# Second layer of the last three token blocks by seven products of halves

## The chip, the cores and the metric

The kernel runs on one core of one Trainium2 chip. A core has five engines with queues of their own: TensorE (PE in the profile; its weight loads are listed apart as PEld), VectorE (DVE), ScalarE (ACT), GpSimd (POOL) and SyncE (SP, here only DMA issues). TensorE multiplies into PSUM, which has 8 banks of 2 KB in each of 128 partitions; the other engines work on SBUF, and VectorE and ScalarE on PSUM too. Each engine takes its queue in order; semaphores hold an instruction back until what it depends on is done. The metric is device time in microseconds (us), less is better.

## The reference

Two stages follow each other: an attention over 8 batches, 8 heads, 576 positions and 64 columns a head, and a feed-forward pair of matrices over the 4608 x 512 tokens that come out of it.

```
q_d, k_d, v_d = means of 4 neighbouring positions          # 144 coarse positions
out_up    = repeat(softmax(q_d k_d^T / 8) v_d, 4)          # coarse attention
out_local = softmax(q k^T / 8 where |i - j| < 4) v         # band attention
x = (out_up + out_local) as 4608 tokens x 512
h = x @ w_in                                               # 512 -> 2048
g = where(h > 0, h, exp(min(h, 0)) - 1)
out = g @ w_out                                            # 2048 -> 512
```

## The kernel before, in words

All matmul operands are fp16, sums are fp32. The tokens are cut into 9 blocks of 512 (t = 0 to 8). A batch of attention has 576 tokens, so the attention of batch b feeds blocks b and b + 1 in part; batch 7 feeds the last 64 tokens of block 7 and the whole of block 8.

For a block, the first layer is `mm1(t, i)`, i = 0 to 15: four matmuls of 512 columns (line 719) make 128 of the 2048 hidden features for the 512 tokens in one PSUM bank called hp. ScalarE takes exp of it (line 723), VectorE turns that into min(e, 1) - 1 (line 724) and adds max(h, 0) from the bank (line 725); the result is one of 16 slices of the tile gt. There are two hp banks. The second layer is `mm2(t, i)`, i = 0 to 15: four matmuls of 512 columns each (line 739), sixteen for each quarter of 128 tokens, which add up in a bank of the tag misc (two banks). ScalarE copies the quarter to an os tile (line 745), and SP sends it out (line 747). The last quarter of block 8 is made in two parts of 384 and 128 columns.

The attention of a batch works on four pairs of heads (j = 0 to 3). GpSimd casts the loaded q, k and v to fp16 (lines 241, 302) and sums q; TensorE transposes q (line 328) and makes scores (lines 458, 471) in two-bank tiles called two0, two1 (and two2 at the front); ScalarE takes their exps (line 481), VectorE masks them (line 496) and sums k (line 377); TensorE adds up denominators (line 518), then makes the outputs lg (lines 602, 622), again in two-bank tiles. VectorE multiplies them by the reciprocals (lines 666, 671), and GpSimd adds the coarse part and writes the block's input xt (line 683).

The order of all of this is written out by hand. Every piece of work is put on a list with a time (`at(time, fn, ...)`), the list is sorted by time, and the pieces are issued in that order; each engine's queue thus has the order of the list, and the times have no other meaning. `mm1_at(t, i)` is i steps behind the start of block t, and blocks start 16 steps apart; `mm2_at(t, i)` is half a step behind `mm1_at(t + 1, i)`. So from block 3 on TensorE alternates between four matmuls of the first layer of block t + 1 and four of the second layer of block t, and the pieces of the attention lie between them at offsets given for each batch (the tables LATER, and LAST for batch 7). The second layer of block 8 has nothing beside it.

PSUM is full: two banks misc, two hp, four in two0 and two1. SBUF is one pool, sb.

## Time and profile before

| | |
|---|---|
| median of 3 runs | 352.85 us |
| lowest, highest run | 350.0, 353.14 us |
| profiled execution: span from the first to the last instruction | 353.6 us |
| TensorE busy | 335.8 us (95%) |
| VectorE, ScalarE, GpSimd busy | 236.2, 180.6, 160.0 us |
| mean granted TensorE clock | 0.981 |
| first layer, line 719 | 512 matmuls, 133.7 us busy |
| second layer, line 739 | 592 matmuls, 146.0 us busy |

Busy time is the time in which an engine has an instruction under way. Matmuls overlap in the pipeline, so the time of one (some 380 ns for 512 columns) is longer than the distance between two; distances are read from starts. In the order of time, "x4" is a merged row of four like instructions, whose length reaches from the first start to the last end; what stands in brackets is the engine's idle time before it and what ended it. "L719" is line 719 of the kernel before.

### The profile page before, as it was taken

How to read it: one execution, taken by the hardware profiler on the slowest of the kernel's cores; microseconds unless marked ns; L12 is line 12 of the kernel's file. 1: busy time of each engine (PE TensorE's matmuls, PEld its weight loads, DVE VectorE, ACT ScalarE, POOL GpSimd, SP SyncE). 2: the span in 40 equal slices, each digit the busy share in tenths (PEclk: the TensorE clock that was granted, in tenths of full speed). 3: DMA queues.
4: the chain of work that ended last, by engine and by line, in shares of the span. 5: the costliest groups of instructions: out<-in, count | busy, mean ns of one | idle time of the engine just before them, and what ended most of it. 6: DMA issues, size and time to landing. Idle time of an engine off the chain costs nothing.

```text
span 353.6 us, 10486 instructions
## 1 busy us (share of the span) xinstructions
PE 335.8 (95%) x4288; PEld 185.3 (52%) x4288; DVE 236.2 (67%) x466; ACT 180.6 (51%) x312; POOL 160.0 (45%) x298
## 2 busy tenths in 40 slices
PE   8897998899889998899999999999999999999996
PEld 4665784455455544445555555545455544444443
DVE  2316999665878775977797789779756955555510
ACT  3572795256665653466355636663553444444421
POOL 4563458286875841973396449755300600000000
PEclk9998999879989999999999999999999999999999
DMA  9999997899998869898979797953014010010012
GB/s 177 201 209 192 213 208 152 200 213 190 188 185 158 167 139 181 168 190 158 196 150 214 158 214 155 168 131 54 30 35 116 32 59 31 32 52 37 32 59 89
DMA packets 98768, 48.89 MB, mean 138 GB/s; under 512 B 81617, under 2 KB 93217, under 8 KB 98721
## 3 DMA queue, kind: packets, MB, share of 16 engines
q1 hardware_dynamic: 94417, 41.86, 58.7%
q0 software_dynamic: 4064, 6.26, 10.0%
q8 instruction: 33, 0.54, 0.7%
q10 hardware_dynamic: 240, 0.11, 0.2%
q14 instruction: 14, 0.11, 0.1%
HBM read 41.97 MB, written 9.55 MB: 146 GB/s over the span
## 4 chain that ended last, share of the span: by engine, by line
PE 75%; DVE 13%; DMA 6%; issue 3%; ACT 3%; SPq 0%; DVEq 0%; ACTq 0%
PE op L739 31%; PE hp L719 28%; DVE gt L725 4%; DMA rcb<-rd 3%; DVE e L724 3%; DVE ln L671 2%; DMA rd<-rc 2%; PE sc L758 2%; PE tqk L328 2%; PE sc L458 2%; PE lg L602 1%; ACT e L723 1%; PE vs L405 1%; PE lg L622 1%; PE den L518 1%
## 5 line engine op out<-in xcount | busy, mean ns | idle before, releaser
L739 PE MATMUL op<-WO,gt 128*128 128x512 f16 (+2 forms) x592 | 146.0, 375 | 0.5 <-DVE gt L725 0.5
L723 ACT ACTIVATE e<-hp 128x512 f16<-128x512 f32 x144 | 86.2, 599 | 107.1 <-PE hp L719 95.3
L719 PE MATMUL hp<-xt,WI 128*128 128x512 f16 x512 | 133.7, 385 | 1.4 <-DVE gt L725 1.3
L725 DVE SCALAR_TENSOR_TENSOR gt<-hp,e 128x512 f16<-128x512 f32 x144 | 99.6, 692 | 6.4
L724 DVE TENSOR_SCALAR e<-e 128x512 f16<-128x512 f16 x144 | 60.6, 421 | 58.4 <-ACT e L723 58.0
L739 PEld LDWEIGHTS <-gt 128*128 128x128 f16 x592 | 55.4, 98 | 61.7 <-issue 1.6
L719 PEld LDWEIGHTS <-WI 128*128 128x128 f16 x512 | 55.6, 115 | 50.0 <-issue 3.2
L683 POOL TENSOR_TENSOR xt<-ln 128x128 f16<-128x128 f16 (+7 forms) x55 | 36.6, 693 | 56.9 <-DVE ln L671 56.9
L481 ACT ACTIVATE pex<-sc 128x580 f16<-128x580 f32 (+1 forms) x56 | 30.1, 594 | 9.2 <-PE sc L471 8.6
L302 POOL CAST v<-v 128x640 f16<-128x640 f32 (+1 forms) x32 | 23.7, 741 | 20.4 <-DMA v<-in_v_dram 13.6
L394 POOL TENSOR_TENSOR t<-qt 128x288 f32<-128x288 f16 x27 | 18.1, 670 | 31.4 <-ACT qt L358 31.4
L745 ACT COPY os<-op 128x512 f32<-128x512 f32 (+2 forms) x37 | 21.4, 578 | 18.9 <-PE op L739 18.8
L377 DVE TENSOR_REDUCE ke<-kt 128x145 f16<-128x580 f16 x28 | 21.0, 751 | 2.4 <-ACT kt L365 2.4
L358 ACT COPY qt<-tqk 128x576 f16<-128x576 f16 x28 | 17.9, 639 | 8.4 <-PE tqk L328 7.7
L671 DVE TENSOR_TENSOR ln<-lg,rcb 128x580 f16<-128x580 f32 x28 | 21.1, 752 | 0.0
L241 POOL CAST k<-k 96x768 f16<-96x768 f32 x24 | 19.8, 825 | 0.1
L241 POOL CAST q<-q 96x768 f16<-96x768 f32 x24 | 19.6, 818 | 0.0
L698 PE MATMUL hp<-xt,WI 128*128 128x256 f16 x128 | 17.0, 283 | 0.7 <-DVE v L276 0.4
L496 DVE TENSOR_TENSOR pex<-pex,MASK 128x580 f16<-128x580 f16 x28 | 13.6, 486 | 3.0 <-ACT pex L481 2.8
L698 PEld LDWEIGHTS <-WI 128*128 128x128 f16 x128 | 13.3, 116 | 1.9 <-issue 0.8
L396 POOL TENSOR_TENSOR qd<-t 128x144 f16<-128x144 f32 x27 | 12.1, 448 | 2.1
L458 PEld LDWEIGHTS <-kt 64*64 64x64 f16 x560 | 6.9, 109 | 11.2 <-issue 8.6
(113 smaller groups left out, 273.4 us busy)
## 6 DMA issues: line engine op xcount, KB each, us to landing
out_dram<-os SPq DMA_DIRECT2D x35, 256.0 KB, 2.1
v<-in_v_dram SPq DMA_DIRECT2D x111, 80.0 KB, 4.5
q<-in_q_dram SPq DMA_DIRECT2D x25, 288.0 KB, 3.9
...
```

The source lines that it names most:

```text
L241: nc.gpsimd.tensor_copy(out=x[:], in_=src)
L302: nc.gpsimd.tensor_copy(out=v16[:], in_=v32[:].rearrange("p (e c) d -> p c e d", e=2))
L481: nc.scalar.activation(out=s["p"][:, :, a : a + n], in_=g2(sc, a, n), func=AF.Exp, scale=SCALE / 16 if a else SCALE,)
L671: nc.vector.tensor_tensor(out=ln[:, 0 : 2 * WL].rearrange("p (m h u) -> p m h u", h=2, u=WQ), in0=_free(lg[:, 0:1], [[WQ, WM], [512, 2], [ ...
L683: eng.tensor_tensor(out=xt(t)[:, j, t0 - TBLK * t : t1 - TBLK * t], in0=ln[:, a:z], in1=_rep4(ln[:, ga : ga + (z - a) // 4]), op=AB.add,)
L698: nc.tensor.matmul(FS[i][:, 256 * f : 256 * f + 256], w_in(dc, 2 * n + f), xts[0][:, dc, 256 * h : 256 * h + 256], start=(f == dc == 0), s ...
L719: nc.tensor.matmul(hp, w_in(dc, fc), xts[t][:, dc, :], start=(dc == 0), stop=(dc == DMC - 1),)
L723: nc.scalar.activation(out=e, in_=hp, func=AF.Exp)
L724: nc.vector.tensor_scalar(out=e, in0=e, scalar1=1.0, scalar2=-1.0, op0=AB.min, op1=AB.add)
L725: nc.vector.scalar_tensor_tensor(out=to, in0=hp, scalar=0.0, op0=AB.max, in1=e, op1=AB.add)
L739: nc.tensor.matmul(op_[:, a:z], gts[t][:, fc, 128 * tt : 128 * tt + 128], WO[:, fc, a:z], start=(fc == 0), stop=(fc == FCN - 1),)
L745: nc.scalar.copy(out=os_[:, a:z], in_=op_[:, a:z])
```

## The change

For the blocks t = 6, 7 and 8 (SW = 6) the second layer is made in another way. The block's 512 x 2048 activations g are taken as 2 x 2 halves, by tokens (256) and hidden features (1024), and w_out as 2 x 2 halves by hidden features (1024) and columns (256). Seven products of halves, with sums and differences of the halves as factors, give the four quarters of the output (Winograd's form of Strassen's scheme) where eight products would be needed:

- `weights_7`: four differences of the halves of w_out, in eight VectorE subtractions of 128 x 1024 fp16 elements, listed from 0.6 steps after the last casts of batch 7, every 2 steps.
- `sums_7(t, g)`: four sums and differences of the halves of g for a quarter g of the features, 128 x 512 elements each, on GpSimd (the last group of block 8 on VectorE). One of the four is written in place in gt. They are listed behind `mm1(t, 4 g + 3)`; the third group of block 6 stands behind the last outputs of batch 7. So that both halves of the features come together, the first layer of these blocks makes slices 0, 8, 1, 9, ...
- `product(t, u, n)`: eight matmuls of 256 columns for 128 of the 256 tokens of a half (u = 0, 1). Products 1, 6, 5 and 3 add up in the left half of a bank y, one after the other, and what stands there in between is read by ScalarE (copies after 1 and 6) and VectorE; products 2, and 7 and 4, go to the two halves of a misc bank.
- `finish(t, u, n)`: after products 4 and 5 a VectorE addition, after 3 a ScalarE copy, make the output rows, and SP sends them.

For blocks 6 and 7 the products stand in the order 1, 2, 7, 6, 4, 5, 3 at 0, 1, 2, 3, 4, 5 and 7 steps of each half block, the finishes of 4 and 5 0.6 steps behind, that of 3 0.1 steps behind. For block 8 they follow each other directly.

In blocks 7 and 8, ten of sixteen slices (i % 8 in BELOW) get their activation from two ScalarE instructions, r = Relu(-h) and e = Exp(-r), and one of VectorE, max(e - 1, h).

When the last outputs of batch 7 are made, the banks of two0 and two1 go back (`close_attention`) and become two banks y and two banks hx; hx takes half of the slices of the first layer of blocks 7 and 8. The SBUF tiles that are needed up to the last casts and transposes of batch 7 are in two pools of their own (lo, tu), which are closed there (`close_feed`, `close_turn`); the differences, sums and output tiles take their place.

```
+SW = 6
+BELOW = (1, 2, 5, 6, 7)
...
+    feed = ctx.enter_context(ExitStack())
+    turn = ctx.enter_context(ExitStack())
+    lo = feed.enter_context(tc.tile_pool(name="lo", bufs=1, side="right"))
+    tu = turn.enter_context(tc.tile_pool(name="tu", bufs=1))
...
+    pairs_ = ctx.enter_context(ExitStack())
+    tp = pairs_.enter_context(tc.tile_pool(name="tp", bufs=1, space=bass.MemoryType.PSUM))
+    fp = front.enter_context(tc.tile_pool(name="fp", bufs=1, space=bass.MemoryType.PSUM, side="right"))
     late = {}
...
     def bank(tag, name):
-        pool = late["ps"] if tag == "hp" else ps
+        pool = {"hp": late["ps"], "misc": ps}.get(tag) or late["end"]
         return pool.tile([128, 512], FP32, tag=tag, bufs=2, name=name)
...
-    def mm1(t, fc):
+    def mm1(t, i):
+        fc = i if t < SW else i // 2 + 8 * (i % 2)
         if fc == 0:
             gts[t] = sb.tile([128, FCN, TBLK], FP16, tag="gt", bufs=2, name="gt")
         e = sb.tile([128, TBLK], FP16, tag="e", bufs=3, name="e")[:]
             h, n = divmod(fc, 8)
             to = gts[t][:, 2 * n : 2 * n + 2, 256 * h : 256 * h + 256]
         else:
-            hp, to = bank("hp", "hp")[:], gts[t][:, fc, :]
+            hp = bank("hx" if t > SW and i % 4 > 1 else "hp", "hp")[:]
+            to = gts[t][:, fc, :]
             for dc in range(DMC):
                 nc.tensor.matmul(
                     hp, w_in(dc, fc), xts[t][:, dc, :],
                     start=(dc == 0), stop=(dc == DMC - 1),
                 )
+        if t > SW and i % 8 in BELOW:
+            r = sb.tile([128, TBLK], FP32, tag="os", bufs=3, name="r")[:]
+            nc.scalar.activation(out=r, in_=hp, func=AF.Relu, scale=-1.0)
+            nc.scalar.activation(out=e, in_=r, func=AF.Exp, scale=-1.0)
+            nc.vector.scalar_tensor_tensor(
+                out=to, in0=e, scalar=-1.0, op0=AB.add, in1=hp, op1=AB.max
+            )
+            return
         nc.scalar.activation(out=e, in_=hp, func=AF.Exp)
         nc.vector.tensor_scalar(out=e, in0=e, scalar1=1.0, scalar2=-1.0, op0=AB.min, op1=AB.add)
         nc.vector.scalar_tensor_tensor(
 
     def mm2(t, i):
         tt, part = i // 4, i % 4
-        cols = ((0, DM),)
-        if t == NT - 1 and tt == 3:
-            cols, part = ((0, 384), (384, DM)), 0
-        for a, z in cols:
-            if part == 0:
-                ops[(t, tt)] = bank("misc", "op")
-            op_ = ops[(t, tt)]
-            for fc in range(4 * part, 4 * part + 4 if len(cols) == 1 else FCN):
-                nc.tensor.matmul(
-                    op_[:, a:z], gts[t][:, fc, 128 * tt : 128 * tt + 128], WO[:, fc, a:z],
-                    start=(fc == 0), stop=(fc == FCN - 1),
-                )
-            if part == 3 or len(cols) == 2:
-                os_ = sb.tile([128, DM], FP32, tag="os", bufs=3, name="os")
-                nc.scalar.copy(out=os_[:, a:z], in_=op_[:, a:z])
-                r = TBLK * t + 128 * tt
-                nc.sync.dma_start(out=out[r : r + 128, a:z], in_=os_[:, a:z])
+        if part == 0:
+            ops[(t, tt)] = bank("misc", "op")
+        op_ = ops[(t, tt)]
+        for fc in range(4 * part, 4 * part + 4):
+            nc.tensor.matmul(
+                op_[:], gts[t][:, fc, 128 * tt : 128 * tt + 128], WO[:, fc, :],
+                start=(fc == 0), stop=(fc == FCN - 1),
+            )
+        if part == 3:
+            os_ = sb.tile([128, DM], FP32, tag="os", bufs=3, name="os")
+            nc.scalar.copy(out=os_[:], in_=op_[:])
+            r = TBLK * t + 128 * tt
+            nc.sync.dma_start(out=out[r : r + 128], in_=os_[:])
...
+    W7, S7, U7 = {}, {}, {}
+    MH, TH, FH = DM // 2, TBLK // 2, FCN // 2
+    def close_feed():
+        feed.close()
+        late["w"] = ctx.enter_context(tc.tile_pool(name="w7", bufs=1, side="right"))
+        W7["T"] = late["w"].tile([128, 4, FH, MH], FP16, tag="T", name="w7")
+    def close_turn():
+        turn.close()
+        late["s"] = ctx.enter_context(tc.tile_pool(name="s7", bufs=1))
+    def weights_7(n, c):
+        T, k = W7["T"], slice(4 * c, 4 * c + 4)
+        b11, b12 = WO[:, k, 0:MH], WO[:, k, MH:DM]
+        b21, b22 = WO[:, FH + 4 * c :, 0:MH][:, 0:4], WO[:, FH + 4 * c :, MH:DM][:, 0:4]
+        x, y = ((b12, b11), (b22, T[:, 0, k]), (b22, b12), (b21, T[:, 1, k]))[n]
+        nc.vector.tensor_tensor(out=T[:, n, k], in0=x, in1=y, op=AB.subtract)
+    def sums_7(t, g):
+        if g == 0:
+            S7[t] = late["s"].tile([128, 3, FH, TH], FP16, tag="S", bufs=2, name="s7")
+        S, G, k, l = S7[t], gts[t], slice(2 * g, 2 * g + 2), slice(FH + 2 * g, FH + 2 * g + 2)
+        a11, a12, a21, a22 = G[:, k, 0:TH], G[:, l, 0:TH], G[:, k, TH:TBLK], G[:, l, TH:TBLK]
+        eng = nc.vector if (t, g) == (NT - 1, 3) else nc.gpsimd
+        for to, x, y, op in (
+            (S[:, 0, k], a21, a22, AB.add), (a21, a11, a21, AB.subtract),
+            (S[:, 1, k], S[:, 0, k], a11, AB.subtract), (S[:, 2, k], a12, S[:, 1, k], AB.subtract),
+        ):
+            eng.tensor_tensor(out=to, in0=x, in1=y, op=op)
+    def close_attention():
+        pairs_.close()
+        late["end"] = ctx.enter_context(tc.tile_pool(name="end", bufs=1, space=bass.MemoryType.PSUM))
+    def unit(t, u):
+        if (t, u) not in U7:
+            z, y = bank("misc", "xz"), bank("y", "y")
+            sn = late["s"].tile([128, 3, MH], FP32, tag="sn", bufs=2, name="sn")
+            ou = late["s"].tile([128, 2, DM], FP32, tag="ou", bufs=2, name="ou")
+            U7[(t, u)] = z, y, sn, ou
+        return U7[(t, u)]
+    def product(t, u, n, k0=0, k1=FH):
+        xz, y, sn, ou = unit(t, u)
+        G, S, T = gts[t], S7.get(t), W7["T"]
+        a, b = slice(128 * u, 128 * u + 128), slice(TH + 128 * u, TH + 128 * u + 128)
+        to = y[:, 0:MH] if n in (1, 3, 5, 6) else xz[:, 0:MH] if n == 2 else xz[:, MH:DM]
+        for k in range(k0, k1):
+            w, x = (
+                (G[:, k, a], WO[:, k, 0:MH]), (G[:, FH + k, a], WO[:, FH + k, 0:MH]),
+                (S[:, 2, k, a], WO[:, FH + k, MH:DM]), (G[:, FH + k, b], T[:, 3, k]),
+                (S[:, 0, k, a], T[:, 0, k]), (S[:, 1, k, a], T[:, 1, k]), (G[:, k, b], T[:, 2, k]),
+            )[n - 1]
+            nc.tensor.matmul(
+                to, w, x, start=(k == 0 and n in (1, 2)), stop=(k == FH - 1),
+                skip_group_check=n > 2,
+            )
+        if k1 == FH and n in (1, 6, 7):
+            nc.scalar.copy(out=sn[:, {1: 0, 6: 1, 7: 2}[n], :], in_=to)
+    def finish(t, u, n):
+        xz, y, sn, ou = unit(t, u)
+        to = y[:, 0:MH]
+        r, z = TBLK * t + 128 * u, TBLK * t + TH + 128 * u
+        if n == 4:
+            nc.vector.tensor_tensor(
+                out=ou[:, :, 0:MH], in0=xz[:].rearrange("p (c m) -> p c m", c=2), in1=sn[:, 0:2, :],
+                op=AB.add,
+            )
+        if n == 5:
+            nc.vector.tensor_tensor(out=ou[:, 1, MH:DM], in0=to, in1=sn[:, 2, :], op=AB.add)
+            nc.sync.dma_start(out=out[z : z + 128], in_=ou[:, 1, :])
+            if (t, u) == (NT - 1, 1):
+                nc.sync.dma_start(out=out[r : r + 128, 0:MH], in_=ou[:, 0, 0:MH])
+        if n == 3:
+            nc.scalar.copy(out=ou[:, 0, MH:DM], in_=to)
+            m0 = MH if (t, u) == (NT - 1, 1) else 0
+            nc.sync.dma_start(out=out[r : r + 128, m0:DM], in_=ou[:, 0, m0:DM])
...
-            if 16 * t + i <= 16 * NT - 4:
+            if t < SW:
                 at(mm2_at(t, i), mm2, t, i)
+    at(PLAN[B - 1]["cast"][3] + 0.05, close_feed)
+    at(PLAN[B - 1]["tr"][3] + 0.05, close_turn)
+    for n in range(4):
+        for c in range(2):
+            at(PLAN[B - 1]["cast"][3] + 0.6 + 2 * (2 * n + c), weights_7, n, c)
+    for t in range(SW, NT):
+        for g in range(4):
+            x = mm1_at(t, 4 * g + 3) + 0.05
+            if (t, g) == (SW, 2):
+                x = max(x, max(PLAN[B - 1]["out"]) + 0.1)
+            at(x, sums_7, t, g)
+        z = mm2_at(t, 0)
+        if t < NT - 1:
+            for u in range(2):
+                for n, x in zip((1, 2, 7, 6, 4, 5, 3), (0, 1, 2, 3, 4, 5, 7)):
+                    at(z + 8 * u + x, product, t, u, n)
+                    if n in (4, 5, 3):
+                        at(z + 8 * u + x + (0.1 if n == 3 else 0.6), finish, t, u, n)
+        else:
+            steps = [(u, n, 0, FH - 1) for u in range(2) for n in (1, 2)]
+            steps += [(u, n, FH - 1, FH) for u in range(2) for n in (1, 2)]
+            steps += [(u, n) for u, n in ((0, 7), (0, 6), (1, 7), (1, 6), (0, 4), (0, 5), (1, 4), (1, 5), (0, 3), (1, 3))]
+            for n, x in enumerate(steps):
+                at(z + n, product, t, *x)
+                if x[1] in (4, 5, 3):
+                    at(z + n + 0.1, finish, t, *x)
+    at(mm1_at(SW + 1, 0) - 0.1, close_attention)
```

More of the change, by code (lines that the diff above doesn't have):

```diff
@@ L120, in const @@
     def const(a, name, queue):
-        t = C[name] = sb.tile(list(a.shape), FP16, tag=name, bufs=1, name=name)
+        pool = sb if name in ("ID", "MASK", "IND2", "VR2") else lo
+        t = C[name] = pool.tile(list(a.shape), FP16, tag=name, bufs=1, name=name)
         queue.dma_start(out=t[:], in_=nc.inline_tensor(a, name=name + "c").ap())
+    feed = ctx.enter_context(ExitStack())
+    turn = ctx.enter_context(ExitStack())
+    lo = feed.enter_context(tc.tile_pool(name="lo", bufs=1, side="right"))
+    tu = turn.enter_context(tc.tile_pool(name="tu", bufs=1))
     front = ctx.enter_context(ExitStack())
     ps = ctx.enter_context(tc.tile_pool(name="ps", bufs=1, space=bass.MemoryType.PSUM))
-    fp = front.enter_context(tc.tile_pool(name="fp", bufs=1, space=bass.MemoryType.PSUM))
+    pairs_ = ctx.enter_context(ExitStack())
+    tp = pairs_.enter_context(tc.tile_pool(name="tp", bufs=1, space=bass.MemoryType.PSUM))
+    fp = front.enter_context(tc.tile_pool(name="fp", bufs=1, space=bass.MemoryType.PSUM, side="right"))
     late = {}
@@ L136, in two @@
         turns.append(turns.pop(0))
-        pool = fp if turns[-1] == 2 else ps
+        pool = fp if turns[-1] == 2 else tp
         return pool.tile([128, 1024 if dt == FP32 else 2048], dt, tag=f"two{turns[-1]}", bufs=1, name=name)
     def bank(tag, name):
-        pool = late["ps"] if tag == "hp" else ps
+        pool = {"hp": late["ps"], "misc": ps}.get(tag) or late["end"]
         return pool.tile([128, 512], FP32, tag=tag, bufs=2, name=name)
@@ L147, in close_front @@
         late["ps"] = ctx.enter_context(
-            tc.tile_pool(name="late", bufs=1, space=bass.MemoryType.PSUM)
+            tc.tile_pool(name="late", bufs=1, space=bass.MemoryType.PSUM, side="right")
         )
@@ L175, in load_wo @@
         nc.gpsimd.dma_start(out=WO[:, 4 * n : 4 * n + 4, :], in_=src)
-    KD = [sb.tile([128, 2 * KG + 16], FP16, tag=f"kd{i}", bufs=1, name="kd") for i in range(4)]
+    KD = [lo.tile([128, 2 * KG + 16], FP16, tag=f"kd{i}", bufs=1, name="kd") for i in range(4)]
     KE = [sb.tile([128, 192], FP16, tag=f"ke{i}", bufs=1, name="ke") for i in range(4)]
@@ L244, in cast_qk @@
         qk16[(b, j)] = got[:: 1 if b < FLIP else -1]
-    V00 = sb.tile([KW, 2 * NB, D], FP32, tag="v32", bufs=3, name="v32")
+    V00 = lo.tile([KW, 2 * NB, D], FP32, tag="v32", bufs=3, name="v32")
     def load_v(b, j):
@@ L253, in load_v @@
             return
-        t = V00 if (b, j) == (0, 0) else sb.tile([KW, 2 * NB, D], FP32, tag="v32", bufs=3, name="v32")
+        t = V00 if (b, j) == (0, 0) else lo.tile([KW, 2 * NB, D], FP32, tag="v32", bufs=3, name="v32")
         def part(p0, p1, i0, i1):
@@ L272, in load_windows @@
     def load_windows(b, j, a):
-        t = sb.tile([128, 2 * WM, D], FP32, tag="v32", bufs=3, name="v32")
+        t = lo.tile([128, 2 * WM, D], FP32, tag="v32", bufs=3, name="v32")
         if b == 1:
@@ L391, in sums @@
         else:
-            t2 = sb.tile([128, 2 * SD], FP32, tag="pex", bufs=2, name="t2")
+            t2 = tu.tile([128, 2 * SD], FP32, tag="pex", bufs=2, name="t2")
             at_ = src.rearrange("p (g f) -> p f g", f=2)
@@ L750 @@
     act, dve = nc.scalar.copy, nc.vector.tensor_copy
-    Z = sb.tile([128, 512], FP16, tag="Z", bufs=1, name="Z")
+    Z = lo.tile([128, 512], FP16, tag="Z", bufs=1, name="Z")
     def keep(t, n):
@@ L826, in selections @@
         else:
-            src = sb.tile([KW, 16], FP16, tag="I4", bufs=1, name="I4")
+            src = lo.tile([KW, 16], FP16, tag="I4", bufs=1, name="I4")
             nc.vector.tensor_reduce(
@@ L830, in selections @@
             )
-            t = C[name] = sb.tile([KW, 1024], FP16, tag=name, bufs=1, name=name)
+            t = C[name] = lo.tile([KW, 1024], FP16, tag=name, bufs=1, name=name)
             parts, step = ((0, 8, 0),), 8
```

12 lines of the change are left out of this document (6 added, 6 removed).

## The prediction

> **What bounds the kernel now.** I read the page's busy times first, then the stretches of the last third, then the order of time in one steady step.
>
> ```profile
> PE 335.8 (95%) x4288; PEld 185.3 (52%) x4288; DVE 236.2 (67%) x466; ACT 180.6 (51%) x312; POOL 160.0 (45%) x298
> ```
>
> TensorE (PE) leads, but a share of the whole span says nothing of blocks 6 to 8, so I cut the end into stretches. The columns are PE, weight load, VectorE (DVE), ScalarE (ACT), GpSimd (POOL), then the granted clock.
>
> ```profile
> 240.00:260.00 20.00, 19.94 (x258) 10.39 (x258) 16.27 (x32) 10.15 (x18) 7.64 (x12) 1.00 0.12 42
> 260.00:281.50 21.50, 21.50 (x286) 11.19 (x285) 15.37 (x31) 8.82 (x15) 5.16 (x8) 1.00 0.23 62
> 281.50:309.10 27.60, 27.60 (x130) 13.46 (x129) 15.84 (x33) 11.91 (x20) 0.16 (x1) 1.00 0.10 39
> 309.10:336.70 27.60, 27.60 (x129) 13.44 (x128) 15.75 (x33) 11.91 (x20) 0.00 (x0) 1.00 0.10 39
> 336.70:353.60 16.90, 14.03 (x81) 7.15 (x79) 0.97 (x2) 3.09 (x6) 0.00 (x0) 1.00 0.21 78
> ```
>
> The reader should see that PE has no gap from 260 to 336.7 us, at full clock, while POOL is idle from 281.5 on. Whatever shortens PE there shortens the kernel, and any new wait on PE lengthens it by its full length: nothing is left to absorb it.
>
> ```profile
> 268.88 1.03 PE L719 MATMUL hp<-xt,WI 128*128 128x512 f16 x4
> 269.74 1.03 PE L739 MATMUL op<-WO,gt 128*128 128x512 f16 x4
> 269.94 0.60 ACT L723 ACTIVATE e<-hp 128x512 f16<-128x512 f32 x1 [1.13 <-PE hp L719]
> 270.57 0.29 DVE L724 TENSOR_SCALAR e<-e 128x512 f16<-128x512 f16 x1 [0.71 <-ACT e L723]
> 270.61 1.03 PE L719 MATMUL hp<-xt,WI 128*128 128x512 f16 x4
> 270.90 0.69 DVE L725 SCALAR_TENSOR_TENSOR gt<-hp,e 128x512 f16<-128x512 f32 x1
> 281.46 0.81 PE L719 MATMUL hp<-xt,WI 128*128 128x512 f16 x3
> 334.99 1.03 PE L719 MATMUL hp<-xt,WI 128*128 128x512 f16 x4
> ```
>
> One step is four first-layer and four second-layer matmuls: 270.61 - 268.88 = 1.73 us, 0.865 for each four, 0.216 for a matmul of 512 columns. Activation starts 0.20 after the four end. The last first-layer step, mm1(8,15), starts at 334.99; 31 steps of 1.727 earlier, at 281.46, is mm1(7,0), from which the second layer of block 6 follows.
>
> **Term 1, fewer columns.** A block's second layer goes from 64 matmuls of 512 columns to 7 products x 8 matmuls x 2 halves = 112 of 256. What one of 256 costs has two neighbours in the trace.
>
> ```profile
> 51.06 1.06 PE L698 MATMUL hp<-xt,WI 128*128 128x256 f16 x8
> L698 PE MATMUL hp<-xt,WI 128*128 128x256 f16 x128 | 17.0, 283 | 0.7 <-DVE v L276 0.4 <-DVE gt L725 0.3
> 350.01 0.50 PE L739 MATMUL op<-WO,gt 128*128 128x128 f16 x6
> L739 PE MATMUL op<-WO,gt 128*128 128x128 f16 x16 | 1.1, 219 | 0.0
> L698 PEld LDWEIGHTS <-WI 128*128 128x128 f16 x128 | 13.3, 116 | 1.9 <-issue 0.8
> L739 PEld LDWEIGHTS <-gt 128*128 128x128 f16 x592 | 55.4, 98 | 61.7 <-issue 1.6
> ```
>
> L698's eight follow each other every (1.06 - 0.28) / 7 = 0.111 us, with weight loads of 116 ns; the products load from gt-like tiles (98 ns). The 128-column ones follow every (0.50 - 0.219) / 5 = 0.056, closer than a load is long, so loads overlap. Between 0.056 and 0.216, halfway by columns, lies 0.109, which I take: 112 x 0.109 = 12.2 against 64 x 0.216 = 13.8, so 1.6 a block and **-4.8 us** in three (ends: 0.108, which is half of 0.216, gives -5.2; 0.111 gives -4.2). The Trainium skill speaks against small matmuls: TensorE: Matmul & The Clock Gate, section Back-to-back issue gap, gives about 81 ns for 128 columns and 131 for 512 in a stream with its loads. By an estimate between them (98 ns) the change would lose 112 x 98 - 64 x 131 = 2.6 us a block; the 56 and 216 ns above contradict both figures, so it gets no chance.
>
> **Term 2, product 3 waits for its own bank.** This is the step on which I decide. Products 1, 6, 5 and 3 add up in one bank y, and VectorE's finish of product 5 must read y before product 3 writes it. By their times, product 5 is queued at step 5.5 of a half block, mm1 of step 6 at 6.0, that finish at 6.1, mm1 of step 7 at 7.0, product 3 at 7.5 (step 6.5 has no product). VectorE takes its queue in order, so the finish stands behind the activation of step 6. Step 6 (and 14, in the second half) is one of those that now go through two ScalarE instructions before VectorE's. From the end of its matmuls: 0.20 to ScalarE, 0.60 for Relu and 0.60 for Exp (as L723), 0.69 for VectorE, then the finish. That has 256 columns from PSUM:
>
> ```profile
> L671 DVE TENSOR_TENSOR ln<-lg,rcb 128x580 f16<-128x580 f32 x28 | 21.1, 752 | 0.0
> L666 DVE TENSOR_TENSOR ln<-lg,rcb 128x144 f16<-128x144 f32 x28 | 8.4, 300 | 6.2 <-DMA rcb<-rd 3.9 <-PE lg L622 2.2
> ```
>
> (752 - 300) / 436 = 1.04 ns a column, so 300 + 112 x 1.04 = 416 ns. The chain is 0.20 + 0.60 + 0.60 + 0.69 + 0.42 = 2.5, and PE has only mm1 of step 7 (0.865) to cover it: 1.65, with the hand-over to PE 1.7 us of idle PE. Queued behind it on PE is everything else: mm1 of the next step, then all products. It happens twice in block 6 and twice in block 7: **+6.8** (ends 6.0, if the two ScalarE instructions take 0.5 each, and 8.0, if a copy of 0.3 stands ahead of them). Block 8's products come with no mm1 between, its finishes directly behind them with two other products (1.7 us) as cover against 0.2 + 0.42: no wait.
>
> **Term 3, product 7 of block 6 waits for POOL.** The last sums of block 6 are queued on POOL behind the last additions of the attention.
>
> ```profile
> 279.00 2.66 POOL L683 TENSOR_TENSOR xt<-ln 128x64 f16<-128x64 f16 x4 [1.84 <-DVE ln L671]
> L683 POOL TENSOR_TENSOR xt<-ln 128x512 f16<-128x512 f16 x4 | 4.3, 1070 | 0.0
> L302 POOL CAST v<-v 128x640 f16<-128x640 f32 x28 | 20.4, 729 | 12.6 <-DMA v<-in_v_dram 12.5
> 274.50 2.66 POOL L683 TENSOR_TENSOR xt<-ln 128x64 f16<-128x64 f16 x4 [18.88 <-DVE ln L671]
> 275.22 0.75 DVE L724 TENSOR_SCALAR e<-e 128x512 f16<-128x512 f16 x1
> ```
>
> POOL is free at 281.66. Each group of sums is four instructions of 512 elements, 1.07 each; product 7's seventh matmul needs the second of the last group, so six: 281.66 + 6.42 = 288.1. Beside POOL's work L724 takes 0.75 instead of 0.29 (last two rows): one of the two waits for the other. Two L724 in that time cost POOL up to 0.6: 288.7. PE reaches that matmul at 281.46 + 3 x 0.865 + 2 x 0.87 + 6 x 0.109 = 286.45: **+2.3**. Ends: 0, if a two-input sum went at the one-input rate of L302 (0.58, six end at 285.2); 3.0, if more L724 get between. Blocks 7 and 8 are covered: POOL's 4.3 us a group fits four steps of 1.73 twice over. Of this lock the Trainium skill says (SBUF — State Buffer, Who interferes with whom) that VectorE in a two-port mode, or with two SBUF inputs, shares one port pair with GpSimd and the later one waits for the whole instruction. The 0.75 agrees; by it the subtractions of term 4 wait too.
>
> **Term 4, the weights' differences on VectorE.** Eight subtractions of 1024 elements, placed at steps between mm1(5,12) and mm1(6,10). Nearest row:
>
> ```profile
> L496 DVE TENSOR_TENSOR pex<-pex,MASK 128x580 f16<-128x580 f16 x28 | 13.6, 486 | 3.0 <-ACT pex L481 2.8
> 242.73 0.76 DVE L724 TENSOR_SCALAR e<-e 128x512 f16<-128x512 f16 x1
> 246.34 1.03 PE L739 MATMUL op<-WO,gt 128*128 128x512 f16 x4
> 246.68 0.69 DVE L725 SCALAR_TENSOR_TENSOR gt<-hp,e 128x512 f16<-128x512 f32 x1
> 247.43 1.02 PE L719 MATMUL hp<-xt,WI 128*128 128x512 f16 x4
> 248.02 0.69 DVE L725 SCALAR_TENSOR_TENSOR gt<-hp,e 128x512 f16<-128x512 f32 x1
> 249.15 1.03 PE L719 MATMUL hp<-xt,WI 128*128 128x512 f16 x4
> ```
>
> 486 ns for 580 elements makes at most 0.86 for 1024; with a fixed part of 0.15 (L666: 300 - 144 x 1.04) it is 0.74. The first comes ahead of the L724 at 242.73, the second ahead of the L725 at 248.02. PE already waits at 247.43 for the L725 that ends at 247.37, so the first goes through whole, 0.74; the second finds 249.15 - 248.71 = 0.44 of slack: 0.3 more. The other six meet VectorE's gap of 0.71 a step; where block 6's first sums keep POOL busy they overfill it a little, 0.3 in all. **+1.3** (ends 0 and 2.5).
>
> **Term 5, the end.** The last copy has 256 columns, between these, and its transfer 128 KB.
>
> ```profile
> 349.92 0.48 ACT L745 COPY os<-op 128x384 f32<-128x384 f32 x1 [2.01 <-PE op L739]
> 350.81 0.27 ACT L745 COPY os<-op 128x128 f32<-128x128 f32 x1 [0.41 <-PE op L739]
> out_dram<-os SPq DMA_DIRECT2D x9, 256.0 KB, 2.0
> out_dram<-os SPq DMA_DIRECT2D x1, 64.0 KB, 1.5
> ```
>
> 0.375 for 0.27, and 1.65 for 1.5: **+0.25** (0.1 to 1, if the transfers before it are still running).
>
> **At nothing:** the four single-bank tiles, since PE waits for no bank from 260 on (the rows above); ScalarE's extra Relu and small copies, 13 x 0.6 + 4 x 0.38 = 9.3 us in the 13.8 of eight steps; VectorE has less, not more, after 281.5. If their cover went, it would show as PE waiting for hp.
>
> The **sum** is -4.8 + 6.8 + 2.3 + 1.3 + 0.25 = +5.9 us. On this execution, whose span is 353.6 us, that is 359.5; the median of the runs is 0.7 below that span, so I forecast **358.8**. By the terms' ends, not all at once, 355 to 362.5.
>
> **Rivals.** (a) Product 3 doesn't wait. Its place is y, its price the whole of term 2, and it decides at 0.865 us: if VectorE reached the finish before mm1 of step 6, as its 0.71 of idle time a step would allow, the chain is 0.2 + 0.42 and hidden. Then -0.9: 351.9, not slower. Against it stands only the order of the queue. Chance 0.10. (b) Beside that, POOL and VectorE also hide terms 3 and 4, as their half-idle rows after 260 suggest: -4.5, 348.3, faster. Against: both are busy just before 281.5. 0.08. (c) The new gaps make the clock drop. It did so here after gaps:
>
> ```profile
> 66.00:67.00 1.00, 0.55 (x28) 0.41 (x27) 1.00 (x3) 0.00 (x0) 0.00 (x0) 1.00 0.78 167
> 69.00:70.00 1.00, 1.00 (x29) 0.59 (x29) 0.00 (x0) 0.00 (x0) 0.96 (x2) 0.50 1.07 228
> ```
>
> After a stretch with PE 55% busy the granted clock is 0.50. The wait of 2.3, with 1.7 following, is such a stretch; 3.4 us at half clock would add 1.7, twice 3.4: about 361 to 363. 0.12. (d) 256-column matmuls cost so much more than 0.111 that nothing is saved: inside the main range unless over 0.123. Left to the forecast with its range: 0.70.
>
> **Numbers.** 1% is 3.5 us, about what a measurement of this kernel can tell from no change (its three runs lie 3.1 apart): faster is below 349.3, slower above 356.4. Faster has (b), 0.08; within 1% has (a) and 0.08 of the main case, where terms 3 and 4 both come out near zero (353 to 356.4): 0.18; slower the rest, 0.74. The range takes in the main case and one drop of the clock and leaves out (a) and (b): 352.8 to 363.
>
> **What would show it.** PE idle four times for 1.5 to 2 us before product 3, released by VectorE's addition; once for about 2.3 at a product 7, released by POOL; starts of product matmuls 0.109 apart; block 8's second layer 12.2 long with no gap. If PE stays gapless from 281 on, terms 2 and 3 are wrong and the time is (b)'s.

## The result, and the profile after

The changed kernel is slower: its median is 362.92 us (four runs, 361.57 to 363.74) against 351.48 for the kernel before beside it (four runs, 350.0 to 353.14). The ratio is 1.0339, with a 95% interval of 1.0277 to 1.04. The forecast was 358.8, +5.9 on 352.85; slower was right, and the time lies just inside the range, but the loss is about twice the forecast. The ratios here and in the table of the experiments leave out every run that is over 1.5% above the fastest of its kernel, while the medians take in all runs; of e9 that leaves only the two shortest of six, so there the median is the better figure.

The page of the kernel after, busy times of the engines:

```profile
PE 330.9 (91%) x4416; PEld 196.3 (54%) x4416; DVE 253.5 (70%) x470; ACT 193.8 (54%) x343; POOL 211.6 (58%) x342
```

TensorE is busy for 4.9 us less, and the span is 8.4 longer (362.0 against 353.6). The stretches of the last third, with the same columns as before the change:

```profile
240.00:260.00 20.00, 18.62 (x225) 9.42 (x224) 18.30 (x33) 8.63 (x16) 8.67 (x12) 1.00 0.22 44
260.00:282.00 22.00, 22.00 (x313) 11.41 (x312) 21.25 (x35) 9.87 (x17) 13.01 (x12) 1.00 0.25 73
282.00:314.00 32.00, 28.09 (x182) 18.46 (x181) 19.03 (x30) 17.81 (x33) 24.57 (x24) 1.00 0.07 26
314.00:345.00 31.00, 26.93 (x179) 18.34 (x178) 17.61 (x28) 19.88 (x38) 19.39 (x17) 1.00 0.09 34
345.00:362.00 17.00, 13.26 (x120) 11.63 (x119) 5.04 (x11) 3.85 (x10) 0.00 (x0) 1.00 0.26 94
```

PE had no gap from 260 to 336.7 us; now it is idle for 1.4 us before 260, 3.9 from 282 to 314 and 4.1 from 314 to 345. The granted clock is 1.00 throughout in this execution. Where the gaps are is read from the order of time (start, length, engine, line; in brackets the idle time before and what ended it):

```profile
240.22 1.03 PE L730 MATMUL hp<-xt,WI 128*128 128x512 f16 x4
...
250.04 1.08 DVE L784 TENSOR_TENSOR w<-WO 128x1024 f16<-128x1024 f16 x1
250.18 1.02 PE L730 MATMUL hp<-xt,WI 128*128 128x512 f16 x4 [0.86 <-DVE gt L744]
...
285.00 1.03 PE L730 MATMUL hp<-xt,WI 128*128 128x512 f16 x4
...
291.32 1.15 POOL L797 TENSOR_TENSOR gt<-gt 128x512 f16<-128x512 f16 x1
...
292.52 0.39 PE L823 MATMUL xz<-w,gt 128*128 128x256 f16 x2 [2.37 <-POOL gt L797]
...
297.96 1.89 PE L730 MATMUL hp<-xt,WI 128*128 128x512 f16 x8
...
299.03 0.60 ACT L736 ACTIVATE r<-hp 128x512 f32<-128x512 f32 x1 [0.48 <-PE hp L730]
299.19 0.68 DVE L836 TENSOR_TENSOR ou<-xz,sn 128x512 f32<-128x512 f32 x1
299.65 0.63 ACT L737 ACTIVATE e<-r 128x512 f16<-128x512 f32 x1
300.32 0.69 DVE L738 SCALAR_TENSOR_TENSOR gt<-e,hp 128x512 f16<-128x512 f16 x1 [0.45 <-ACT e L737]
300.92 0.42 DVE L841 TENSOR_TENSOR ou<-y,sn 128x256 f32<-128x256 f32 x1
301.39 1.03 PE L823 MATMUL y<-WO,s 128*128 128x256 f16 x8 [1.54 <-DVE ou L841]
...
345.56 1.03 PE L823 MATMUL y<-WO,s 128*128 128x256 f16 x8 [1.54 <-DVE ou L841]
346.43 0.93 PE L823 MATMUL y<-WO,gt 128*128 128x256 f16 x7
...
355.16 1.04 PE L823 MATMUL xz<-w,gt 128*128 128x256 f16 x8
356.04 1.04 PE L823 MATMUL y<-w,s 128*128 128x256 f16 x8
356.91 1.91 PE L823 MATMUL y<-WO,s 128*128 128x256 f16 x16
```

The reader should see, from the top: at 240.22 mm1(5,11), a first-layer step ahead of the first new instruction, for comparison below; the subtractions of the weights delay a first-layer step; product 7 of block 6 waits 2.37 us for GpSimd; and product 3 waits 1.54 us for VectorE's finish of product 5 (L841), which stands behind the activation of the step before (L736, L737, L738), as term 2 had it. Lines of "who waited" for L841 say how often:

```profile
L841 DVE TENSOR_TENSOR ou<-y,sn x6: 417/418/425, 300.9 to 357.1; 128x256 f32<-128x256 f32 x6
  PE y L823: 6.2, 4
```

Four times, 6.2 us; counted from the start that it would have had behind the eight matmuls from 297.96 on, at 0.217 each (299.70), it comes 1.69 late each time. From 346.43 on, block 8's products run without a gap: 12.39 us to the end of the last one at 358.82, where the old second layer took 14.03.

How much of the loss lies where is read from the starts of the same steps in both executions. The kernel before has mm1(5,11) here:

```profile
238.27 1.03 PE L719 MATMUL hp<-xt,WI 128*128 128x512 f16 x4
```

From mm1(5,11) to mm1(7,0), at 281.46 before and 285.00 after, it is 43.19 before and 44.78 after, +1.59, nearly all of it at the two waits behind the subtractions (0.86 at 250.18 and 0.52 at 252.59). From there to the last end on PE (350.73 and 358.82) it is 69.27 before and 73.82 after, +4.55. With 0.3 more at the end (3.1 us from the last matmul to the end of the span against 2.8), what can be seen from 240 us on comes to +6.4. The remaining 2.0 of the 8.4 between the two spans lie in the first 240 us, in which every engine has the same instructions in the same order in both kernels, and only the addresses of tiles differ. The medians differ by 11.4, so 3 us more than these two executions; the two profiles can't place those.

### The profile page after: what moved, and what is told of

It is laid out like the page before. It is cut to its first block, busy times and chain, and to the rows that moved or that the text cites. A ratio compares the mean times of both kernels' runs of the same rounds, so it can differ in the third digit from the quotient of the medians.

```text
span 362.0 us, 10845 instructions
## 1 busy us (share of the span) xinstructions
PE 330.9 (91%) x4416; PEld 196.3 (54%) x4416; DVE 253.5 (70%) x470; ACT 193.8 (54%) x343; POOL 211.6 (58%) x342
## 4 chain that ended last, share of the span: by engine, by line
PE 66%; DMA 12%; DVE 10%; ACT 4%; POOL 3%; SPq 2%; issue 2%; DVEq 0%; POOLq 0%; ACTq 0%
PE hp L730 25%; PE op L754 19%; DMA v<-in_v_dram 6%; PE y L823 6%; PE xz L823 4%; DMA IND<-INDc 3%; DVE ln L680 2%; DVE e L743 2%; DVE gt L744 2%; DMA rcb<-rd 2%; PE sc L467 2%; PE tqk L337 2%; PE lg L611 1%; POOL s L797 1%; ACT e L742 1%
## 5 line engine op out<-in xcount | busy, mean ns | idle before, releaser
L742 ACT ACTIVATE e<-hp 128x512 f16<-128x512 f32 x124 | 74.1, 598 | 89.7 <-PE hp L730 78.6
L754 PE MATMUL op<-WO,gt 128*128 128x512 f16 x384 | 100.4, 385 | 0.0
L743 DVE TENSOR_SCALAR e<-e 128x512 f16<-128x512 f16 x124 | 64.6, 521 | 43.1 <-ACT e L742 42.4
L744 DVE SCALAR_TENSOR_TENSOR gt<-hp,e 128x512 f16<-128x512 f32 x124 | 85.8, 692 | 5.7
L730 PEld LDWEIGHTS <-WI 128*128 128x128 f16 x512 | 55.3, 115 | 47.9 <-issue 6.5
L754 PEld LDWEIGHTS <-gt 128*128 128x128 f16 x384 | 35.8, 99 | 40.9 <-issue 3.0
L797 POOL TENSOR_TENSOR s<-gt 128x512 f16<-128x512 f16 x11 | 13.3, 1213 | 21.9 <-DVE gt L744 10.8
L823 PEld LDWEIGHTS <-gt 128*128 128x128 f16 x192 | 18.7, 98 | 8.0 <-POOL gt L797 2.7
L738 DVE SCALAR_TENSOR_TENSOR gt<-e,hp 128x512 f16<-128x512 f16 x20 | 13.7, 687 | 13.2 <-ACT e L737 12.7
L823 PEld LDWEIGHTS <-s 128*128 128x128 f16 x144 | 14.1, 98 | 10.8 <-issue 7.3
L707 PE MATMUL hp<-xt,WI 128*128 128x256 f16 x128 | 17.9, 288 | 1.3 <-DMA WI<-in_moe_w_in_dram 0.6
```

What stands on the lines that cost most here:

```text
L730: nc.tensor.matmul(hp, w_in(dc, fc), xts[t][:, dc, :], start=(dc == 0), stop=(dc == DMC - 1),)
L742: nc.scalar.activation(out=e, in_=hp, func=AF.Exp)
L743: nc.vector.tensor_scalar(out=e, in0=e, scalar1=1.0, scalar2=-1.0, op0=AB.min, op1=AB.add)
L744: nc.vector.scalar_tensor_tensor(out=to, in0=hp, scalar=0.0, op0=AB.max, in1=e, op1=AB.add)
L754: nc.tensor.matmul(op_[:], gts[t][:, fc, 128 * tt : 128 * tt + 128], WO[:, fc, :], start=(fc == 0), stop=(fc == FCN - 1),)
L823: nc.tensor.matmul(to, w, x, start=(k == 0 and n in (1, 2)), stop=(k == FH - 1), skip_group_check=n > 2,)
```

## The experiments

Two theories can explain the excess over the prediction's terms: the new addresses (the pools lo, tu and tp, and the other side for fp and late) cost time by themselves; or they don't, and the excess is the spread between executions, or a cost of the second layer that the first profile doesn't show. Beside them the terms are tested one by one. Each kernel below was timed beside the kernel before, in three sets on three chips (e1 to e4, e5 to e8, e9 to e12); the table gives medians, the ratio, and a difference that needs a few sentences. Each timed run lists the mean granted clock of its execution, from 0.957 to 0.995 for the kernel before alone, and the times follow it: 0.995 gave 349.2 to 352.5 us, 0.976 gave 353.9 to 357.6. A straight line through the 187 runs of the three sets below, with one slope and a level of its own for each kernel, has a slope of 2.76 us for 0.01 of the clock (standard error 0.15) and a scatter of 1.3 us. "At equal clock" is a kernel's level on it less that of the kernel before, with the standard error. It is a fit, not a measurement with the clock held; a level of its own for each set moves no difference by more than 0.2.

| kernel | runs | median, us | before, us | ratio (95%) | at equal clock, us |
|---|---|---|---|---|---|
| e1: order of before, addresses of after | 12 | 354.66 | 351.78 | 1.0083 (1.0043 to 1.0124) | +1.5 (0.4) |
| e2: finishes earlier | 10 | 354.93 | 351.78 | 1.0062 (1.0014 to 1.0109) | +2.1 (0.4) |
| e3: subtractions later | 4 | 361.80 | 351.78 | 1.0289 (1.0219 to 1.0358) | +9.2 (0.7) |
| e4: last sums of block 6 on VectorE | 4 | 357.65 | 351.78 | 1.0173 (1.0116 to 1.023) | +5.8 (0.7) |
| e5: e2, e3 and e4 together | 10 | 353.71 | 352.26 | 1.004 (1.0 to 1.008) | +1.1 (0.4) |
| e6: SBUF pools alone | 12 | 354.45 | 352.26 | 1.0044 (1.0003 to 1.0084) | +1.7 (0.4) |
| e7: PSUM pools alone | 12 | 352.29 | 352.26 | 0.9977 (0.9937 to 1.0018) | -0.2 (0.4) |
| e8: e5, block 6 on ScalarE too | 10 | 349.50 | 352.26 | 0.9937 (0.9905 to 0.9969) | -2.4 (0.4) |
| e9: the changed kernel again | 6 | 363.09 | 353.02 | 1.0175 (1.0086 to 1.0264) | +9.1 (0.5) |
| e10: pool lo alone | 12 | 354.50 | 353.02 | 1.0058 (1.0022 to 1.0094) | +2.0 (0.4) |
| e11: pool tu alone | 12 | 351.67 | 353.02 | 0.9945 (0.99 to 0.999) | +0.1 (0.4) |
| e12: one ScalarE instruction in steps 6, 14 | 2 | 362.34 | 353.02 | 1.0286 (1.0204 to 1.0368) | +10.9 (0.9) |

**The addresses alone.** e1 is the kernel before with the pools of the changed kernel and SW = 9, so that no block takes the new second layer: on every engine the same instructions in the same order as before.

```diff
+SW = 9
...
+    lo = feed.enter_context(tc.tile_pool(name="lo", bufs=1, side="right"))
+    tu = turn.enter_context(tc.tile_pool(name="tu", bufs=1))
...
+    tp = pairs_.enter_context(tc.tile_pool(name="tp", bufs=1, space=bass.MemoryType.PSUM))
+    fp = front.enter_context(tc.tile_pool(name="fp", bufs=1, space=bass.MemoryType.PSUM, side="right"))
```

> The schedule of before, instruction for instruction on every engine, with only the new division of SBUF and PSUM into pools (other addresses). The changed kernel's trace is 1.95 us late already at mm1(5,11), before its first new instruction. Theory A, the new addresses cost time in the first 240 us: 2 to 5 us slower than before (353.5 to 357). Theory B, the front varies from execution to execution by itself and the profiles of the two kernels fell differently: within 1 us of before (350 to 353).

It took 2.9 us more by the medians, 1.5 at equal clock, as theory A expected. The addresses alone make the kernel slower. e6 keeps only the SBUF part (tp = ps, and fp and late on their old side), e7 only the PSUM part (lo = tu = sb).

> The schedule of before with the SBUF tiles divided into the three pools, PSUM as before. If the 0.8% of the first experiment comes from SBUF addresses: 1.006 to 1.010 of before. If from the PSUM banks: 0.998 to 1.002.

> The schedule of before with the PSUM banks divided as in the changed kernel, SBUF in one pool as before. If the 0.8% of the first experiment comes from the PSUM banks: 1.006 to 1.010 of before. If from SBUF addresses: 0.998 to 1.002.

The SBUF part costs 2.2 us (1.7 at equal clock), the PSUM part nothing; the ratio of e6, 1.0044, is below the 1.006 that was expected at least, with an interval that takes it in. e10 and e11 divide the SBUF part: in e10 only lo is a pool of its own (loaded q, k and v in fp32, most constants and some small tiles), in e11 only tu (the fp16 copies of q and k).

> The schedule of before, with only the tiles of the pool lo (the loaded fp32 q, k, v and constants) at other addresses. If the cost of the SBUF division is in the loads into these tiles: 1.004 to 1.008 of before. If it is in the pool tu (the fp16 copies of q and k that are transposed): 0.998 to 1.002.

> The schedule of before, with only the tiles of the pool tu (the fp16 copies of q and k, and the sums of q) at other addresses. If the cost of the SBUF division is here: 1.004 to 1.008 of before. If it is in the pool lo: 0.998 to 1.002.

It is lo: 1.5 us by the medians, 2.0 at equal clock, while tu costs nothing. (The ratio of e11, 0.9945, is below what was expected; its mean clock was higher, 0.989 against 0.985, and at equal clock +0.1 is left.) The tiles that stay in sb can move too when lo's leave it, so e10 shows which division costs, not which tile. The three kernels with lo at the new place and the old order agree, 1.5, 1.7 and 2.0. So the first theory holds, for lo, but for 2 us of the 5 that the medians have beyond the 6.4. The cost lies in the first 240 us: in all six profiled executions with the order of before (before, e1, e6, e7, e10, e11), mm1(7,0) comes 43.18 to 43.19 us behind mm1(5,11), and the last end on PE 69.27 behind that. What changes there is seen in the DMA issues of the pages (KB each, median us from issue to landing). The page of the kernel before:

```profile
v<-in_v_dram SPq DMA_DIRECT2D x111, 80.0 KB, 4.5
q<-in_q_dram SPq DMA_DIRECT2D x25, 288.0 KB, 3.9
```

The page of the kernel after:

```profile
v<-in_v_dram SPq DMA_DIRECT2D x111, 80.0 KB, 5.1
q<-in_q_dram SPq DMA_DIRECT2D x25, 288.0 KB, 4.8
```

The v loads land in 4.5 to 4.9 us in the three profiled executions with lo's tiles at their old addresses (before, e7, e11) and in 4.8 to 5.6 in the eleven with the new ones, so the two ranges touch. GpSimd's cast of v ends its wait on such a load, and PE waits at 50 to 53 us for what follows that cast: 0.23, 1.16 and 1.44 us in the three, and in the eleven 0.98 to 5.70, but for e12, which has no such wait. Not every load shows it (q is at 3.9 to 4.8 with the new addresses, 3.9 to 4.1 with the old). That the later landing carries the 1.5 to 2 us is argued from these rows, and why addresses matter to a transfer stays open.

**Term 2 alone.** e2 lists the finishes of products 4 and 5 half a step earlier, ahead of the next activation:

```diff
-                        at(z + 8 * u + x + (0.1 if n == 3 else 0.6), finish, t, u, n)
+                        at(z + 8 * u + x + 0.1, finish, t, u, n)
```

> The changed kernel with the finishes of products 4 and 5 listed 0.1 steps behind their product instead of 0.6, so that VectorE has them ahead of the activation of the next step. Theory of term 2 (the order of VectorE's queue makes product 3 wait): the four waits of 1.7 us before product 3 fall to 0.2 or less, 6 to 6.5 us less than the changed kernel's 362.9, about 356.6. Rival (something else on the way from product 5 to product 3, such as ScalarE, is late by itself): the waits stay over 1 us each and the time over 360.

The four waits are gone, and with them 8.0 us by the medians (354.93 against 362.92), 7.0 (0.7) at equal clock against e9; 4 x 1.69 = 6.8 was to be had, and 6 to 6.5 had been expected. The order of time of e2, at the place of the first of them:

```profile
294.08 1.89 PE L730 MATMUL hp<-xt,WI 128*128 128x512 f16 x8
294.70 0.69 DVE L738 SCALAR_TENSOR_TENSOR gt<-e,hp 128x512 f16<-128x512 f16 x1 [0.63 <-ACT e L737]
295.31 0.41 DVE L841 TENSOR_TENSOR ou<-y,sn 128x256 f32<-128x256 f32 x1
295.81 1.04 PE L823 MATMUL y<-WO,s 128*128 128x256 f16 x8
```

VectorE now takes L841 before the activation of the second of the two steps, and product 3 follows without a gap. So the order of VectorE's queue was the cause of term 2.

**Term 3 alone.** e4 gives the last group of sums of block 6 to VectorE:

```diff
-        eng = nc.vector if (t, g) == (NT - 1, 3) else nc.gpsimd
+        eng = nc.vector if (t, g) in ((SW, 3), (NT - 1, 3)) else nc.gpsimd
```

> The changed kernel with the last group of block 6's sums on VectorE instead of GpSimd. Theory of term 3 (six sums on GpSimd behind the last additions of the attention make product 7 late): the wait of 2.4 us before product 7's seventh matmul falls under 0.5, and the time is 1.8 to 2.4 us less than the changed kernel's. Rival (VectorE is as late, or holds the shared work up): a wait of over 1 us stays, before product 7 or before the first layer of block 7.

The order of time of e4, at product 7 of block 6 and at the first of the waits of product 3:

```profile
285.47 1.04 PE L823 MATMUL xz<-w,gt 128*128 128x256 f16 x8
...
294.98 1.03 PE L823 MATMUL y<-WO,s 128*128 128x256 f16 x8 [1.54 <-DVE ou L841]
```

The wait of product 7 is gone, the four of product 3 stay at 1.54. It gains 5.3 us by the medians but 3.3 (0.8) at equal clock, more than the 1.8 to 2.4 that were expected; from mm1(7,0) to the last end on PE it takes 71.27, 2.55 less than in the first profile (e9 shows what else goes with that wait). VectorE paid for it out of its idle time: beside GpSimd three of the four sums took it 1.26 to 1.37 us, and alone, in block 8, 0.42.

**Term 4 alone.** e3 lists the eight subtractions 4.4 steps later:

```diff
-            at(PLAN[B - 1]["cast"][3] + 0.6 + 2 * (2 * n + c), weights_7, n, c)
+            at(PLAN[B - 1]["cast"][3] + 5.0 + 2 * (2 * n + c), weights_7, n, c)
```

> The changed kernel with the eight subtractions of the weights 4.4 steps later, behind the outputs of batch 6. Theory of term 4 (VectorE has no time among the outputs of batch 6 and has some behind them): the two waits of PE for the activation, 0.86 and 0.52 us at 250 and 252 us, go, none over 0.3 takes their place, and the time is 1.0 to 1.6 us less than the changed kernel's. Rival (VectorE is short of time anywhere in block 6): the waits move with them and nothing is gained.

Nothing to speak of is gained: 1.1 us by the medians, none at equal clock (+9.2 against +9.1). The waits of 0.86 and 0.52 are gone, and three others come, of which e3's order of time shows the first two:

```profile
263.71 1.02 PE L730 MATMUL hp<-xt,WI 128*128 128x512 f16 x4 [0.48 <-DVE gt L744]
...
268.71 0.99 DVE L784 TENSOR_TENSOR w<-WO 128x1024 f16<-128x1024 f16 x1
269.63 1.24 DVE L743 TENSOR_SCALAR e<-e 128x512 f16<-128x512 f16 x1
...
271.65 1.02 PE L730 MATMUL hp<-xt,WI 128*128 128x512 f16 x4 [0.87 <-DVE gt L744]
```

With the third, 0.96 at 285.55, they make 2.3, and product 7's wait shrinks to 1.67. So the rival of this expectation came true. The reason is VectorE's time: in block 6 its L743, beside GpSimd's sums, takes 1.24 where the prediction's rows have 0.29, and the subtractions find no gap (e8, which takes ten instructions off VectorE there, bears that out). Where they are put is a choice between two full stretches.

**The three together, and a stretch with room.** e5 has the edits of e2, e3 and e4; e8 adds that block 6 too takes the activation with two ScalarE instructions and one of VectorE:

```diff
-        if t > SW and i % 8 in BELOW:
+        if t >= SW and i % 8 in BELOW:
```

> The changed kernel with all three edits at once: finishes of 4 and 5 at 0.1 steps, subtractions of the weights 4.4 steps later, last sums of block 6 on VectorE. If the waits of the terms 2 to 4 are separate costs, what is left of the change is 4.8 us fewer matmul columns, 0.3 at the end, and 2.9 for the new addresses: 1 to 2 us faster than before, 349.5 to 351. Rival, VectorE now has too much around the start of block 7: one or two waits of about 1 us there, 351 to 353.5. If fewer columns gained nothing, 355 or more.

> The kernel with all three edits, and block 6 too takes its activation of ten steps in sixteen through two ScalarE instructions, which leaves out ten of VectorE's instructions (0.29 to 0.75 us each) where it subtracts the weights. If VectorE is short of time in block 6, the waits for the activation between 260 and 286 us that the experiment with the later weights showed (0.48, 0.87, 0.96) fall under 0.3 each and the time is 1 to 2 us less than with the three edits alone. Rival: the longer way through ScalarE, 0.3 us more with only two hp banks in block 6, makes PE wait in its place, and the time is the same or 1 to 3 us more.

e5 still has the three waits for VectorE (0.49, 0.88, 0.96) and is 0.0 to 0.8% slower than the kernel before; its 353.71 misses the forecast of 349.5 to 351 and lies just above its rival's 353.5. e8 has no wait of PE over 0.3 us from 210 us on, and is faster than the kernel before by 0.6% (0.3 to 1.0%), in spite of the addresses: 349.50 us, the best of all. It is 4.2 us below e5 by the medians, 3.5 at equal clock, where 1 to 2 were expected and the three waits make 2.3. The stretches of e8:

```profile
240.00:260.00 20.00, 19.95 (x206) 10.02 (x205) 17.13 (x30) 12.04 (x21) 10.68 (x15) 1.00 0.11 41
260.00:280.00 20.00, 20.00 (x278) 10.47 (x277) 17.13 (x28) 11.78 (x19) 11.81 (x14) 1.00 0.25 67
280.00:310.00 30.00, 30.00 (x204) 20.73 (x202) 23.50 (x34) 20.89 (x41) 21.41 (x19) 1.00 0.12 45
310.00:340.00 30.00, 30.00 (x223) 22.42 (x222) 17.12 (x29) 18.38 (x37) 16.34 (x15) 1.00 0.10 36
```

PE has no gap again. From the 1.7 us that the addresses cost at equal clock to e8's -2.4 it is -4.1, near the -4.6 of terms 1 and 5 (-4.9 and +0.3) without the others. Its profile shows the same: from mm1(7,0) to the last end on PE it takes 64.64 us where the kernel before takes 69.27, 4.6 less.

**The changed kernel again.** e9 is the changed kernel without an edit, for the size of the excess.

> The changed kernel itself, unedited, once more beside the kernel before. Its traces account for 6.5 us from block 5 on, and the experiments on the pools for 1.5 to 3 more; the result was 11. Theory A, the rest lies in the executions of that day and chip (its trace reached the sums of batch 7's values 3 us later than the edited kernels with the same instructions up to there): now 8 to 9.5 us over before, ratio 1.023 to 1.027. Theory B, the change has a further cost of its own that I have not found: 10.5 to 12 over, ratio 1.030 to 1.034.

It is 10.1 us over the kernel before by the medians, between what the two theories expected, and 9.1 (0.5) at equal clock; its runs reach from 356.87 to 364.44. The waits are those of the first profile, but one thing is new. The stretches of e9 around product 7's wait (the second to last three columns are clock, DMA share, GB/s):

```profile
290.00:292.00 2.00, 1.01 (x6) 0.66 (x7) 0.00 (x0) 0.37 (x1) 2.00 (x2) 1.00 0.00 0
292.00:294.00 2.00, 2.00 (x12) 1.22 (x10) 1.06 (x2) 0.82 (x2) 1.20 (x2) 0.58 0.02 4
294.00:296.00 2.00, 2.00 (x9) 1.00 (x8) 0.15 (x1) 0.67 (x2) 1.69 (x2) 0.56 0.01 4
296.00:298.00 2.00, 2.00 (x17) 1.46 (x16) 1.34 (x2) 0.65 (x2) 1.92 (x3) 1.00 0.00 0
```

After the wait the granted clock falls to 0.50 for 3.4 us, from 292.3 to 295.7 (0.58 and 0.56 are means of 2 us), and the order of time of e9 shows what it costs:

```profile
290.99 0.39 PE L823 MATMUL xz<-w,gt 128*128 128x256 f16 x2 [2.38 <-POOL gt L797]
...
292.08 1.66 PE L823 MATMUL y<-w,s 128*128 128x256 f16 x8
...
298.10 1.89 PE L730 MATMUL hp<-xt,WI 128*128 128x512 f16 x8
```

Eight product matmuls take 1.66 instead of 1.04, and from product 7 to the pair of first-layer steps it is 7.11 us, against 292.52 to 297.96, 5.44, in the first profile: 1.67 more for the same work. Of the four profiled executions with this wait of 2.4 us, two had the drop (e9, e2) and two had none (the first profile, e12); none of the other ten, e4 among them, shows a drop behind 150 us. So rival (c) comes true in a part of the executions, and 1.67 in half of them, an estimate from only four, is 0.8 us on average. Of this the Trainium skill says (TensorE: Matmul & The Clock Gate, Part 1: The HAM clock gate) that the activity window which sets the clock runs freely, so that the same kernel meets it at another phase in each run. That one and the same wait drops the clock in two executions of four agrees. The same page (HAM oscillation — how this bites in real kernels) warns of idle gaps over about 3.4 us; here one of 2.4 was enough, in two executions of four.

**A shorter chain before the finish.** In e12 steps 6 and 14 go back to one ScalarE and two VectorE instructions, and steps 4 and 12 take their place.

```diff
-BELOW = (1, 2, 5, 6, 7)
+BELOW = (1, 2, 4, 5, 7)
```

> The changed kernel, in which step 4 instead of step 6 of eight goes through two ScalarE instructions, so that the activation ahead of the finish of product 5 has one ScalarE instruction (0.60) less and one of VectorE (0.29) more. By the chain of term 2 the four waits before product 3 go from 1.54 us idle to 1.2. If the wait were set by something other than this chain, they stay at 1.54.

The waits did not shrink, they grew to 1.68 to 1.90. The order of time of e12 at the first of them:

```profile
296.72 0.60 ACT L742 ACTIVATE e<-hp 128x512 f16<-128x512 f32 x1 [0.48 <-PE hp L730]
296.88 0.69 DVE L836 TENSOR_TENSOR ou<-xz,sn 128x512 f32<-128x512 f32 x1
297.04 1.15 POOL L797 TENSOR_TENSOR s<-gt,s 128x512 f16<-128x512 f16 x1
297.48 0.86 DVE L743 TENSOR_SCALAR e<-e 128x512 f16<-128x512 f16 x1
298.37 0.69 DVE L744 SCALAR_TENSOR_TENSOR gt<-hp,e 128x512 f16<-128x512 f32 x1
298.98 0.41 DVE L841 TENSOR_TENSOR ou<-y,sn 128x256 f32<-128x256 f32 x1
...
299.44 1.03 PE L823 MATMUL y<-WO,s 128*128 128x256 f16 x8 [1.90 <-DVE ou L841]
```

ScalarE is done 0.6 us sooner, but VectorE is still at L836, the finish of product 4, and then L743 runs beside a sum of GpSimd and takes 0.86. The saved ScalarE instruction is paid back by VectorE. The expectation had left both out; the stretched L743 stood in the prediction's own rows (0.75).

## Why the prediction was right and wrong

Slower, with 0.74, was right, and most of the mechanism was as written. That 362.92 still lies in the range, whose upper end is 363, is luck in part: the range reached so far for a drop of the clock, and most of the excess has another source.

- **Term 1** (-4.8): right. A run of eight product matmuls takes 1.04 and one matmul 0.273, so they follow each other every 0.109. (By columns that is a third of the way between the two neighbours, not "halfway"; the figure was right.) Block 8's second layer took 12.39 against 14.03, 1.64 less than before where 1.6 was forecast, so -4.9 in three blocks if 6 and 7 save the same; e8, which has no waits left there, shows 4.6. Rival (d) falls.
- **Term 2** (+6.8): right in place, cause and size. 1.69 us four times, and e2, by the order of the queue alone, took 7.0 (0.7) away. Rival (a) falls with it. The chain is not the only one of that length: e12 shortened it by one ScalarE instruction, and VectorE's own queue (L836, then the stretched L743) made the wait as long again.
- **Term 3** (+2.3): right, 2.4. The six sums took 7.16 us together, 1.15 to 1.20 each and not 1.07, which is about what had been set apart for L724 beside them (7.0 with the 0.6). Rival (b) falls. Blocks 7 and 8 were covered as forecast, though four steps (6.9 us) are 1.6 times a group's 4.3, not twice.
- **Term 4** (+1.3): 1.6 by the starts, nearly all of it at the two waits. The subtraction was mis-sized: the first two took 1.15 and 1.08, beside GpSimd, where 0.74 was taken; alone it took 0.68. The slack that the forecast gave to the other six held. The later place of e3 has no more time for them; with e8's relief of VectorE it has.
- **Term 5** (+0.25): 0.3.

Together these make +6.2, and the profile shows +6.4 from 240 us on, against a sum of +5.9 in the prediction. What failed is the list **"At nothing"**. It put the PSUM tiles there, and e7 bears that out; but the same edit moves the loaded tiles to other SBUF addresses, and that had no row, no price and no bound in the prediction at all. It costs 1.5 to 2.0 us at equal clock (e1, e6, e10), 1.5 to 2.9 by the medians, and the first two profiles differ by 2.0 in the first 240 us. A trace of before can't price it, but a bound of some us could have stood in the range for it. What the list says of VectorE, that it has less to do after 281.5, was wrong too: it is busy for 36.6 of the 63 us from 282 to 345, where it had 31.6 of 55.2. PE still has no wait for hp from there on, so that cost nothing by itself.

The second step that failed is the choice between **rival (c) and the forecast**, which were set against each other with 0.12. The wait of term 3 makes the clock drop in some executions and not in others (two of four), for 1.67 us, just under the 1.7 that (c) gave; it belonged in the sum with half its price, 0.8.

6.4, 1.7 and 0.8 are 8.9, and the medians of the two sets say 11.4 and 10.1. The anchor adds about 1: the sum was put on 352.85, a median of three runs, the fourth brought it to 351.48, and the 81 later runs of the same kernel have a median of 352.43. At equal clock, where the drop is mostly taken out, 6.4 + 1.7 = 8.1 stands against 9.1 (0.5) in e9, and the first four runs lie 8.3 above the line on average. What is left over by the medians goes with the mean clock of the executions: three of the first four runs had 0.981 and one 0.967, where the kernel before has 0.985 on average. Whether the changed kernel causes any of that in its first 240 us, or met it by chance, isn't settled (the first two profiles have equally much time at half clock there, 13.7 us); up to about 1 us at equal clock, which is within two standard errors, stays unexplained.
